# A pre-norm attention and FFN block on one core: spaced weight loads, the row maxima added by GpSimd, and a shorter lag between two passes

## The chip, the cores and the metric

The kernel runs on one core of a Trainium2 chip. The metric is the device time of the program in microseconds. Five engines work side by side, each through its own list in order: TensorE (PE in the profile, its weight loads PEld), VectorE (DVE), ScalarE (ACT), GpSimd (POOL) and SyncE (SP), which here only issues DMA transfers.

## What is computed

The reference, cut to what matters (2048 tokens, width 512, 32 heads of 16, FFN width 1792, all bf16):

```python
h  = x + attention(layernorm(x)) @ wo          # softmax(q k^T / 4) v, 32 heads
h2 = h + (gelu(layernorm(h) @ w_gate) * (layernorm(h) @ w_up)) @ w_down
```

## The kernel before

The kernel is one planned stream. A small planner (`P.op`, `P.dma`) takes the instructions in the order in which the Python code emits them, keeps for each buffer key the last writer and the readers, and puts semaphore waits where an engine needs another's result. Every engine then runs its own list strictly in the order of emission, so an instruction that waits holds up all that was emitted after it for that engine.

**Units and two passes.** The queries are cut in eight groups of 256 rows (`gi`), the heads in eight slots of four heads (`slot`), which makes 64 units. A unit has 16 ticks. In the *first pass* TensorE computes scores of 128 queries by 512 keys into PSUM, two matmuls a tick (`p1_pair`, L573), and VectorE takes the maximum of each row (`p1_consume`, L582). After a unit's last tick `negm_pre` reduces these to one negated maximum for each row and head (NEGM, L588), and GpSimd splits it into three bf16 parts in four short instructions (L592 to L595) that write the tile ST. `negm_post` transposes ST into STG by DMA (L601) and copies three rows for each of the four heads from STG into the spare rows 16 to 18 of that head's block of QT (L604, four transfers). KT holds ones in these rows, so that in the *second pass* the matmul of K by Q (`p2_pair`, L618) yields the score minus the maximum, and ScalarE only has to take the exponential (L628). Matmuls with V follow (`pv_burst`, L644).

**The order of the work.** One loop runs over ticks. In each tick it emits a first-pass pair of unit `tick // 16`, a second-pass pair of unit `(tick - P2_START) // 16`, then either matmuls with V or a piece of the "dense" stream, then what was deferred to this tick. `P2_START = 16 + LAGX`, so a unit's second pass begins LAGX ticks after the last tick of its first pass. The waits of a tick's first-pass and second-pass matmuls are gathered ahead of the first of them: TensorE starts neither before both may run. The loop ends when the second pass does; the last ticks have second-pass work alone.

**The dense stream** holds the QKV projections at the start, the end of each pair of slots (`item_ofin`: GpSimd's reciprocal of the sums, L670, and the scaling, L673), the output projection, and the FFN of each group (`item_gate`, `item_up`, `item_down`). It takes one PSUM bank at a time once `dense.single` is set, four ticks before P2_START; before that it runs at a faster rate. It is started by what the second pass has finished and keeps its own pauses in ticks. Each gate tile is copied out by ScalarE (g), GpSimd makes the inner polynomial of GELU of it (L781 to L783), ScalarE takes its tanh four or more ticks after the copy (L795), GpSimd finishes it (L786, L787) and multiplies by the up tile (L843). Seven such tiles belong to one FFN group; the last group's FFN runs after the loop.

**The FFN weights** lie where the QKV projection's buffers were. When the last projection has been emitted, `qkv_finished` emits three loads (L482 to L484, 1792 KB each) for SyncE, which wait for the readers of the old buffers.

**SyncE** issues all transfers in the order of emission. It knows nothing of ticks: it goes on as soon as the wait of its next transfer is fulfilled.

Of the kernel before, what the change touches and what calls it, by code (L numbers as in the profile page):

```python
# [189 lines left out]
ALU = mybir.AluOpType  # L190
# [6 lines left out]
GC = 0.7978845608028654  # L197

NPT = 12
LAGX = 10  # L200
PAUSE = 2


def bass_sequential_preLN__mha_block__geglu_ffn__prompt_kernel(nc, A_x, A_wqkv, A_wo, B_x, B_w_gate, B_w_up, B_w_down, out):
    dbg = None
    with ExitStack() as es:
        block = es.enter_context(nc.Block())
        P = Plan(nc, es)
# [270 lines left out]
        def qkv_finished():  # L479
            fk = [("xnT", t) for t in range(NT)] + ["wqkv"] + [(nm_, dc) for nm_ in ("wq_r", "wk_r") for dc in range(4)] + [("QKS", i_) for i_ in range(4)] + [("QKS2", i_) for i_ in range(2)]  # L480
            dF = rdeps("F", fk)
            P.dma("sp", lambda e: e.dma_start(out=wg_sb[:], in_=B_w_gate.rearrange("(c p) j -> p c j", p=128)), "wg", writes=["wg"], extra_deps=dF)  # L482
            P.dma("sp", lambda e: e.dma_start(out=wu_sb[:], in_=B_w_up.rearrange("(c p) j -> p c j", p=128)), "wu", writes=["wu"], extra_deps=dF)
            P.dma("sp", lambda e: e.dma_start(out=wd_sb[:], in_=B_w_down.rearrange("(c p) j -> p c j", p=128)), "wd", writes=["wd"], extra_deps=dF)  # L484

        qk_n = [0]
        qk_late = []
        def item_projT(b, which, ht, c):
            wr, nm = (wq_r, "wq_r") if which == "q" else (wk_r, "wk_r")
            for dc in range(4):  # L490
                P.op("pe", lambda e, dc=dc: e.matmul(pbank[:, b, :], wr[:, dc, 128 * ht:128 * ht + 128], xnT[:, dc, 512 * c:512 * c + 512], start=(dc == 0), stop=(dc == 3)),  # L491
                     reads=[(nm, dc)] + [("xnT", t) for t in range(4 * c, 4 * c + 4)], writes=[("pb", b)], sig=(dc == 3))
                if dc == 1:
                    yield 2
            si, s2 = qk_n[0] % 4, qk_n[0] % 2; qk_n[0] += 1
            def dst(slot):
                if which == "q":
                    return QT[:, c, slot, :], [("qT", slot, c)] + [("qTaug", slot, c, f_, g_) for f_ in range(2) for g_ in range(4)]
                return KT[:, slot, 512 * c:512 * c + 512], [("kT", slot, c)]
            def mask_op(src, key, slot):  # L500
                o_ap, keys = dst(slot)
                if which == "q":
                    P.op("pool", lambda e: e.tensor_scalar(out=o_ap, in0=src, scalar1=qmask[:, 0:1], scalar2=None, op0=ALU.mult), reads=[key, "qmask"], writes=keys)  # L503
                else:
                    P.op("pool", lambda e: e.tensor_scalar(out=o_ap, in0=src, scalar1=kmask[:, 0:1], scalar2=kbias[:, 0:1], op0=ALU.mult, op1=ALU.add), reads=[key, "kmask", "kbias"], writes=keys)
            p1_now = p1_begun[0]
            def direct():
                o_ap, keys = dst(2 * ht)
                if which == "q":
                    P.op("act", lambda e: e.activation(out=o_ap, in_=pbank[:, b, :], func=ACT.Copy, scale=qmask[:, 0:1]), reads=[("pb", b), "qmask"], writes=keys)  # L510
# [12 lines left out]
            qkv_left[0] -= 1  # L523
            if qkv_left[0] == 0:
                qkv_finished()
            return 2
# [38 lines left out]
        def p1_pair(ui, j, gp):  # L565
            gi, slot = units[ui]
            c, hf = gi // 2, gi % 2
            qt, kc = 2 * hf + j // 8, (j // 2) % 4
            tiles = []
            for jj in range(2):  # L570
                g = 2 * gp + jj
                b = p1_ring[0] % 3; p1_ring[0] += 1
                P.op("pe", lambda e, g=g, b=b: e.matmul(pbank[:, b, :], QT[32 * g:32 * g + 32, c, slot, 128 * qt:128 * qt + 128],  # L573
                                                        KT[32 * g:32 * g + 32, slot, 512 * kc:512 * kc + 512], start=True, stop=True, tile_position=(32 * g, 0)),
                     reads=[("qT", slot, c), ("qTaug", slot, c, hf, g), ("kT", slot, kc)], writes=[("pb", b)], sig=(jj == 1))
                tiles.append((b, j // 8, kc, g))
            return tiles

# [18 lines left out]
        def negm_post(ui):  # L597
            gi, slot = units[ui]
            c, hf = gi // 2, gi % 2
            par = ui % 2  # L600
            P.dma("sp", lambda e: e.dma_start_transpose(out=STG[:, par, :].rearrange("p (q s) -> p q s", q=2), in_=ST[:, par].rearrange("p q s -> p (q s)")),  # L601
                  ("stT", par), reads=[("ST", par)], writes=[("STG", par)])
            for g in range(4):
                P.dma("sp", lambda e, g=g: e.dma_start(out=QT[32 * g + 16:32 * g + 19, c, slot, 256 * hf:256 * hf + 256], in_=STG[32 * g + 16:32 * g + 19, par, :]),  # L604
                      ("aug", par), reads=[("STG", par)], writes=[("qTaug", slot, c, hf, g)])

        pv_pending = []
        pt_n = [0]
# [1 line left out]
        def p2_pair(ui, j, gp):  # L610
            gi, slot = units[ui]
            c, hf = gi // 2, gi % 2
            m = j // 2
            tiles = [(banks.take(), m, 2 * gp + jj) for jj in range(2)]
            for i in range(2):
                kt = 2 * m + i
                for (b, _, g) in tiles:
                    P.op("pe", lambda e, g=g, b=b, kt=kt, i=i: e.matmul(pbank[:, b, 256 * i:256 * i + 256], KT[32 * g:32 * g + 32, slot, 128 * kt:128 * kt + 128],  # L618
                                                                        QT[32 * g:32 * g + 32, c, slot, 256 * hf:256 * hf + 256], start=True, stop=True, tile_position=(32 * g, 0)),
                         reads=[("qT", slot, c), ("kT", slot, kt // 4)] + [("qTaug", slot, c, hf, g_) for g_ in range(4)], writes=[("pb", b)],  # L620
                         sig=(i == 1 and g == 2 * gp + 1))
            return tiles

# [69 lines left out]
        def add_ffn(gi):  # L693
# [3 lines left out]
            for k in range(2):  # L697
                dense.add(item_down, gi, k, est=7)

        def load_xres(gi):  # L700
            assert gi < 2 or ffn_done.get(gi - 2), "dense stream too far behind (residual reuse)"
            for k in range(2):
                P.dma("sp", lambda e, k=k: e.dma_start(out=g_h(gi, k), in_=xv[:, 2 * gi + k, :]), ("xres", gi % 2, k), writes=[("h", gi % 2, k)])
# [14 lines left out]
        def post_hnT(gi, k):  # L718
# [2 lines left out]
                  ("hnT", 2 * gp + k), reads=[("OH", 2 * gp + k)], writes=[("hnT", gp, k)])  # L721
            hn_left[gi] = hn_left.get(gi, 2) - 1
            if hn_left[gi] == 0:
                defer(3, lambda: add_ffn(gi))

        def item_oproj(b, gi, k):
            gp, t = gi % 2, 2 * gi + k
# [71 lines left out]
        def gate_up_mms(b, gi, f, w, nm):  # L799
            hT = hnT_l[gi % 2]  # L800
            hr = [("hnT", gi % 2, k) for k in range(2)]
            for i in range(2):
                fc = 2 * f + i
                for dc in range(4):
                    P.op("pe", lambda e, dc=dc, fc=fc, i=i: e.matmul(pbank[:, b, 256 * i:256 * i + 256], w[:, dc, 128 * fc:128 * fc + 128], hT[:, dc, :], start=(dc == 0), stop=(dc == 3)),  # L805
                         reads=[nm] + hr, writes=[("pb", b)], sig=(dc == 3 and i == 1))
                if i == 0:
                    yield 2

# [37 lines left out]
        def down_mm(b, gi, k, fc):  # L847
            gp = gi % 2
            P.op("pe", lambda e: e.matmul(pbank[:, b, :], GUT[:, fc, 256 * gp + 128 * k:256 * gp + 128 * k + 128], wd_sb[:, fc, :], start=(fc == 0), stop=False),  # L849
                 reads=[("GUT", fc, gp), "wd"], writes=[("pb", b)], sig=False)  # L850

        def down_last(b, gi, k):
            P.op("pe", lambda e: e.matmul(pbank[:, b, :], ident[:], g_h(gi, k), start=False, stop=True),
# [153 lines left out]
        while True:  # L1007
# [31 lines left out]
            if pv_tick:  # L1039
                pv_burst(8)  # L1040
            run_deferred(tick)
            tick += 1
        run_deferred(tick, flush=True)
        tail_mode[0] = True
# [34 lines left out]
```

## Time and profile before

| | us |
|---|---|
| median of 3 runs | 1392.69 (1392.41 to 1392.97) |
| the profiled execution, whole | 1393.8 |
| its span, from the first to the last instruction | 1392.1 |
| busy: VectorE / ScalarE / TensorE matmul / GpSimd | 1288.5 / 1235.2 / 1080.1 / 585.9 |
| VectorE's L582, 2048 times: busy / idle just before them | 1248.9 / 38.1 |
| ScalarE's L628, 2048 times: busy | 1103.8 |

The page cuts the span into 40 slices and gives the busy share of each engine in tenths. Its chain follows the work back from the last instruction to what released each step. A line of a group names the source line, engine, operation, tiles and shapes, and then busy time, mean duration and idle time of the engine before it with what ended it. A line of a timeline gives the start, the duration, the instruction, how many in a row, and in brackets the idle time before it with its releaser. Transfers show on SP's queue (SPq) with the time that the issue took. TensorE's granted clock was 0.991 of full speed over the span.

### The profile page before, as it was taken

What the parts mean: (1) busy time and instruction counts of PE and PEld (TensorE: products, weight loads), DVE (VectorE), ACT (ScalarE), POOL (GpSimd) and SP (SyncE); (2) the same over time, 40 slices, a digit from 0 to 9 for tenths busy, and PEclk for the clock granted to TensorE, in tenths of its full rate; (3) what the DMA queues carried; (4) which work ended last, traced back from release to release, by engine and by line L of the source; (5) the groups of instructions that cost most, each with busy time, mean ns of one, the idle gap of its engine ahead of it and who ended that gap; (6) DMA issues with size and microseconds to landing.
All of it is one profiled execution on the core that took longest, in us unless ns stands there. A gap on an engine that the chain in (4) does not pass through costs nothing.

```text
span 1392.1 us, 33568 instructions
## 1 busy us (share of the span) xinstructions
PE 1080.1 (78%) x12464; PEld 372.1 (27%) x12682; DVE 1288.5 (93%) x2190; ACT 1235.2 (89%) x2409; POOL 585.9 (42%) x830
## 2 busy tenths in 40 slices
PE   4977757777787778777787778777787778877787
PEld 2222212223222222222222322222222322222224
DVE  5999969999999999999999999999999999999912
ACT  4499959999999999999999999899999999999991
POOL 4446611256313562236422662146512563145611
PEclk9999989999999999999999999999999999999999
DMA  3110040100010000000001000100001000100000
GB/s 121 42 29 24 26 164 6 29 5 4 10 21 17 4 6 13 21 11 6 6 13 26 6 6 9 23 13 6 4 13 29 6 3 10 25 14 3 6 15 12
DMA packets 50096, 28.00 MB, mean 20 GB/s; under 512 B 35600, under 2 KB 48400, under 8 KB 49936
## 3 DMA queue, kind: packets, MB, share of 16 engines
q1 hardware_dynamic: 49936, 25.84, 7.0%
q8 instruction: 103, 1.69, 0.5%
q14 instruction: 57, 0.47, 0.1%
HBM read 11.80 MB, written 2.10 MB: 10 GB/s over the span
## 4 chain that ended last, share of the span: by engine, by line
DVE 72%; PE 10%; ACT 8%; issue 7%; DMA 1%; POOL 1%; SPq 1%; POOLq 0%; ACTq 0%; DVEq 0%
DVE PM L582 70%; ACT PT L628 6%; PE pbank L573 3%; PE pbank L618 2%; PE pbank L644 1%; PE pbank L805 1%; DVE NEGM L588 1%; PE pbank L491 1%; PE pbank L849 1%; DVE stats L324 1%; ACT OA L467 1%; DMA OnT<-Otok 1%; PE pbank L730 1%; SPq L604 0%; DMA STG<-ST 0%
## 5 line engine op out<-in xcount | busy, mean ns | idle before, releaser
L582 DVE TENSOR_REDUCE PM<-pbank 128x1 f32<-128x512 f32 x2048 | 1248.9, 685 | 38.1 <-PE pbank L618 26.1
L628 ACT ACTIVATE PT<-pbank 128x512 bf16<-128x512 f32 x2048 | 1103.8, 613 | 87.1 <-PE pbank L618 24.6
L573 PE MATMUL pbank<-KT,QT 32*128 32x512 bf16 x2048 | 399.8, 383 | 208.8 <-DVE PM L582 148.4
L618 PE MATMUL pbank<-QT,KT 32*128 32x256 bf16 x4096 | 401.0, 273 | 2.3 <-ACT PT L628 2.2
L573 PEld LDWEIGHTS pbank<-KT,QT 32*128 32x128 bf16 x2048 | 109.2, 91 | 592.6 <-DVE PM L582 575.0
L1001 PE MATMUL pbank<-ones_bf,ident 128*128 128x512 bf16 x651 | 213.9, 384 | 36.8 <-ACT PT L628 28.9
L644 PE MATMUL pbank<-PT,VA 128*17 128x256 bf16 x4096 | 203.7, 276 | 18.8
L592 POOL CAST ST<-NEGM 128x8 bf16<-128x8 f32 x64 | 13.9, 218 | 318.6 <-DVE NEGM L588 318.6
L670 POOL TENSOR_TENSOR LINV<-OAT,negone 128x16 f32<-128x16 f32 (+1 forms) x32 | 92.0, 2876 | 92.9 <-ACT OAT L467 67.2
L618 PEld LDWEIGHTS pbank<-QT,KT 32*128 32x128 bf16 x4096 | 114.8, 92 | 11.2 <-ACT PT L628 7.0
L644 PEld LDWEIGHTS pbank<-PT,VA 128*17 128x17 bf16 x4096 | 56.5, 87 | 147.0 <-PE pbank L644 92.4
L781 POOL TENSOR_TENSOR w_sb<-g_sb 128x512 f32<-128x512 f32 x49 | 50.9, 1039 | 105.8 <-ACT g_sb L467 105.8
L1001 PEld LDWEIGHTS pbank<-ones_bf,ident 128*128 128x128 bf16 x826 | 49.8, 97 | 100.5 <-ACT PT L628 68.1
L805 PE MATMUL pbank<-hnT_l,wg_sb 128*128 128x256 bf16 x448 | 67.9, 277 | 1.8 <-issue 0.7
L805 PE MATMUL pbank<-hnT_l,wu_sb 128*128 128x256 bf16 x448 | 67.9, 277 | 0.0
L783 POOL TENSOR_TENSOR w_sb<-w_sb,g_sb 128x512 f32<-128x512 f32 x49 | 62.1, 1268 | 4.1
L787 POOL TENSOR_TENSOR th_sb<-th_sb,g_sb 128x512 f32<-128x512 f32 x49 | 62.0, 1264 | 4.1
L843 POOL TENSOR_TENSOR GUT<-th_sb,u_sb 128x512 bf16<-128x512 f32 x49 | 62.0, 1266 | 0.5
L849 PE MATMUL pbank<-wd_sb,GUT 128*128 128x512 bf16 x202 | 56.1, 381 | 5.5 <-PE pbank L618 2.0
L503 POOL TENSOR_SCALAR QT<-QKS,qmask 128x512 bf16<-128x512 bf16 x31 | 48.2, 1562 | 27.3 <-DMA QKS<-QKS 19.5
L786 POOL TENSOR_SCALAR th_sb<-th_sb 128x512 f32<-128x512 f32 x49 | 30.2, 617 | 68.3 <-ACT th_sb L795 68.3
L805 PEld LDWEIGHTS pbank<-hnT_l,wg_sb 128*128 128x128 bf16 x448 | 36.2, 98 | 27.7 <-issue 14.0
(112 smaller groups left out, 639.2 us busy)
## 6 DMA issues: line engine op xcount, KB each, us to landing
QT<-STG SPq DMA_DIRECT2D x256, 1.5 KB
QKS<-QKS SPq DMA_DIRECT2D x32, 112.0 KB, 2.2
x_sb<-in_A_x_dram SPq DMA_DIRECT2D x4, 512.0 KB, 5.6
xres<-in_A_x_dram SPq DMA_DIRECT2D x16, 128.0 KB, 2.2
out_dram<-out_sb SPq DMA_DIRECT2D x16, 128.0 KB, 1.8
wg_sb<-in_B_w_gate_dram SPq DMA_DIRECT2D x1, 1792.0 KB, 7.2
wu_sb<-in_B_w_up_dram SPq DMA_DIRECT2D x1, 1792.0 KB, 12.1
wd_sb<-in_B_w_down_dram SPq DMA_DIRECT2D x1, 1792.0 KB, 16.6
```

The lines of the kernel that those rows point to most:

```text
L573: P.op("pe", lambda e, g=g, b=b: e.matmul(pbank[:, b, :], QT[32 * g:32 * g + 32, c, slot, 128 * qt:128 * qt + 128], KT[32 * g:32 * g + 32, ...
L582: P.op("dve", lambda e, b=b, qt=qt, kc=kc, g=g: e.tensor_reduce(out=PM[:, par, qt, kc, g:g + 1], in_=pbank[:, b, :], axis=AX.X, op=ALU.max ...
L618: P.op("pe", lambda e, g=g, b=b, kt=kt, i=i: e.matmul(pbank[:, b, 256 * i:256 * i + 256], KT[32 * g:32 * g + 32, slot, 128 * kt:128 * kt + ...
L628: P.op("act", lambda e, b=b, pi=pi: e.activation(out=PT[:, pi, :], in_=pbank[:, b, :], func=ACT.Exp), reads=[("pb", b)], writes=[("PT", pi)])
L644: P.op("pe", lambda e, g=g, kt=kt, pi=pi, slot=slot, i=i, col=col: e.matmul(pbank[32 * g:32 * g + 17, PVB, 256 * col:256 * col + 256], VA[ ...
L670: P.op("pool", lambda e: e.tensor_tensor(out=li, in0=oat4[:, :, :, 16], in1=negone[:, 0:8 * ns].rearrange("p (q h) -> p q h", q=2), op=ALU ...
L783: P.op(eng, lambda e: e.tensor_tensor(out=ws, in0=ws, in1=gs, op=ALU.mult), reads=[("w", par), ("g", par)], writes=[("w", par)])
L787: P.op(eng, lambda e: e.tensor_tensor(out=ts_, in0=ts_, in1=gs, op=ALU.mult), reads=[("th", par), ("g", par)], writes=[("th", par)])
L805: P.op("pe", lambda e, dc=dc, fc=fc, i=i: e.matmul(pbank[:, b, 256 * i:256 * i + 256], w[:, dc, 128 * fc:128 * fc + 128], hT[:, dc, :], st ...
L843: P.op("pool", lambda e: e.tensor_tensor(out=o_ap, in0=shp(ts_), in1=shp(us), op=ALU.mult), reads=[("th", par), ("u", par)], writes=o_keys ...
L849: P.op("pe", lambda e: e.matmul(pbank[:, b, :], GUT[:, fc, 256 * gp + 128 * k:256 * gp + 128 * k + 128], wd_sb[:, fc, :], start=(fc == 0), ...
L1001: P.op("pe", lambda e: e.matmul(pbank[:, b, :], ident[:], ones_bf[:, 0:512], start=True, stop=True), reads=["ident", "ones_bf"], writes=[( ...
```

## The change

Three things change together.

1. `LAGX` is 6 instead of 10.
2. The three weight loads become twelve pieces: four of the gate weights and four of the up weights (448 KB each, one for every 128 rows of the width), and four of the down weights (three of 512 KB and one of 256 KB). `qkv_finished` only lists them. The loop emits one piece at ticks 7, 9, 11 and 13 of a unit until the list is empty. The weights' keys are kept by piece, so that a matmul waits for its own. An FFN group is added to the dense stream only once all pieces are emitted.
3. The four transfers from STG into QT become one GpSimd addition of the STG tile to the unit's 256 columns of QT (128 x 256, bf16). STG is zero outside the three rows of each head, and QT is zero in these rows. The keys of QT are kept by halves of 256 columns.

```diff
-LAGX = 10
+LAGX = 6
...
-            P.dma("sp", ... out=wg_sb[:], in_=B_w_gate..., "wg", writes=["wg"], extra_deps=dF)
-            P.dma("sp", ... out=wu_sb[:], in_=B_w_up..., "wu", writes=["wu"], extra_deps=dF)
-            P.dma("sp", ... out=wd_sb[:], in_=B_w_down..., "wd", writes=["wd"], extra_deps=dF)
+            wviews = [(wg_sb, B_w_gate.rearrange("(c p) j -> p c j", p=128), "wg", 1), (wu_sb, B_w_up.rearrange("(c p) j -> p c j", p=128), "wu", 1),
+                      (wd_sb, B_w_down.rearrange("(c p) j -> p c j", p=128), "wd", 4)]
+            for (w, v, nm, step) in wviews:
+                n = w.shape[1]
+                for k in range(0, n, step):
+                    w_pieces.append((w, v, nm, k, min(n, k + step), dF))
+        def w_piece():
+            w, v, nm, k0, k1, dF = w_pieces.pop(0)
+            P.dma("sp", lambda e: e.dma_start(out=w[:, k0:k1, :], in_=v[:, k0:k1, :]), (nm, k0), writes=[(nm, k) for k in range(k0, k1)], extra_deps=dF)
...
         def negm_post(ui):
...
-            for g in range(4):
-                P.dma("sp", lambda e, g=g: e.dma_start(out=QT[32 * g + 16:32 * g + 19, c, slot, 256 * hf:256 * hf + 256], in_=STG[32 * g + 16:32 * g + 19, par, :]),
-                      ("aug", par), reads=[("STG", par)], writes=[("qTaug", slot, c, hf, g)])
+            q_ap = QT[:, c, slot, 256 * hf:256 * hf + 256]
+            P.op("pool", lambda e: e.tensor_tensor(out=q_ap, in0=q_ap, in1=STG[:, par, :], op=ALU.add), reads=[("STG", par), ("qT", slot, c, hf)], writes=[("qT", slot, c, hf)])
...
+        def add_ffn_when(gi):
+            if w_pieces or qkv_left[0]:
+                defer(1, lambda: add_ffn_when(gi))
+            else:
+                add_ffn(gi)
...
             run_deferred(tick)
+            if w_pieces and tick % 16 in (7, 9, 11, 13):
+                w_piece()
```

More of the change, by code (lines that the diff above doesn't have):

```diff
@@ L481, in qkv_finished @@
             dF = rdeps("F", fk)
-            P.dma("sp", lambda e: e.dma_start(out=wg_sb[:], in_=B_w_gate.rearrange("(c p) j -> p c j", p=128)), "wg", writes=["wg"], extra_deps=dF)
-            P.dma("sp", lambda e: e.dma_start(out=wu_sb[:], in_=B_w_up.rearrange("(c p) j -> p c j", p=128)), "wu", writes=["wu"], extra_deps=dF)
-            P.dma("sp", lambda e: e.dma_start(out=wd_sb[:], in_=B_w_down.rearrange("(c p) j -> p c j", p=128)), "wd", writes=["wd"], extra_deps=dF)
+            wviews = [(wg_sb, B_w_gate.rearrange("(c p) j -> p c j", p=128), "wg", 1), (wu_sb, B_w_up.rearrange("(c p) j -> p c j", p=128), "wu", 1),
[4 more added lines that the diff above has]
+                    w_pieces.append((w, v, nm, k, min(n, k + step), dF))
+        w_pieces = []
+        def w_piece():
+            w, v, nm, k0, k1, dF = w_pieces.pop(0)
+            P.dma("sp", lambda e: e.dma_start(out=w[:, k0:k1, :], in_=v[:, k0:k1, :]), (nm, k0), writes=[(nm, k) for k in range(k0, k1)], extra_deps=dF)
         qk_n = [0]
@@ L497, in dst @@
                 if which == "q":
-                    return QT[:, c, slot, :], [("qT", slot, c)] + [("qTaug", slot, c, f_, g_) for f_ in range(2) for g_ in range(4)]
+                    return QT[:, c, slot, :], [("qT", slot, c, f_) for f_ in range(2)]
                 return KT[:, slot, 512 * c:512 * c + 512], [("kT", slot, c)]
@@ L574, in p1_pair @@
                                                         KT[32 * g:32 * g + 32, slot, 512 * kc:512 * kc + 512], start=True, stop=True, tile_position=(32 * g, 0)),
-                     reads=[("qT", slot, c), ("qTaug", slot, c, hf, g), ("kT", slot, kc)], writes=[("pb", b)], sig=(jj == 1))
+                     reads=[("qT", slot, c, hf), ("kT", slot, kc)], writes=[("pb", b)], sig=(jj == 1))
                 tiles.append((b, j // 8, kc, g))
@@ L619, in p2_pair @@
                                                                         QT[32 * g:32 * g + 32, c, slot, 256 * hf:256 * hf + 256], start=True, stop=True, tile_position=(32 * g, 0)),
-                         reads=[("qT", slot, c), ("kT", slot, kt // 4)] + [("qTaug", slot, c, hf, g_) for g_ in range(4)], writes=[("pb", b)],
+                         reads=[("qT", slot, c, hf), ("kT", slot, kt // 4)], writes=[("pb", b)],
                          sig=(i == 1 and g == 2 * gp + 1))
@@ L723, in post_hnT @@
             if hn_left[gi] == 0:
-                defer(3, lambda: add_ffn(gi))
+                defer(3, lambda: add_ffn_when(gi))
         def item_oproj(b, gi, k):
@@ L805, in gate_up_mms @@
                     P.op("pe", lambda e, dc=dc, fc=fc, i=i: e.matmul(pbank[:, b, 256 * i:256 * i + 256], w[:, dc, 128 * fc:128 * fc + 128], hT[:, dc, :], start=(dc == 0), stop=(dc == 3)),
-                         reads=[nm] + hr, writes=[("pb", b)], sig=(dc == 3 and i == 1))
+                         reads=[(nm, dc)] + hr, writes=[("pb", b)], sig=(dc == 3 and i == 1))
                 if i == 0:
@@ L849, in down_mm @@
             P.op("pe", lambda e: e.matmul(pbank[:, b, :], GUT[:, fc, 256 * gp + 128 * k:256 * gp + 128 * k + 128], wd_sb[:, fc, :], start=(fc == 0), stop=False),
-                 reads=[("GUT", fc, gp), "wd"], writes=[("pb", b)], sig=False)
+                 reads=[("GUT", fc, gp), ("wd", fc)], writes=[("pb", b)], sig=False)
         def down_last(b, gi, k):
```

## The prediction

> **What bounds the kernel now.** I read the page first, then the chain, then the waits and timelines of the engines where the change acts.
>
> ```profile
> DVE  5999969999999999999999999999999999999912
> DVE 72%; PE 10%; ACT 8%; issue 7%; DMA 1%; POOL 1%; SPq 1%; POOLq 0%; ACTq 0%; DVEq 0%
> L582 DVE TENSOR_REDUCE PM<-pbank 128x1 f32<-128x512 f32 x2048 | 1248.9, 685 | 38.1 <-PE pbank L618 26.1
> ```
>
> VectorE carries the chain with the 2048 maxima of the first pass (0.61 us each, two a tick: a tick is 1.2 us). A lull of VectorE between the first and last of them is lost for good; there are 38.1 us of these. The 6 in the sixth slice is the largest.
>
> ```profile
> 177.09 12.04 DVE L582 TENSOR_REDUCE PM<-pbank 128x1 f32<-128x512 f32 x20
> 200.30 1.29 DVE L582 TENSOR_REDUCE PM<-pbank 128x1 f32<-128x512 f32 x2 [11.17 <-PE pbank L618]
> ```
>
> ```profile
> 178.68 0.50 SPq L484 DMA_DIRECT2D wd_sb<-in_B_w_down_dram  x1
> 179.28 10.83 SPq L601 DMA_TRANSPOSE STG<-ST  x1
> 195.68 2.86 SPq L604 DMA_DIRECT2D QT<-STG  x4
> ```
>
> The first is VectorE's timeline, the second SyncE's. Behind 5,376 KB of weights, unit 6's transpose lands at 195.68 instead of 2.35 us after its issue; its second pass waits, and the first pass, next in TensorE's order, with it.
>
> The third place is GpSimd around the end of a unit with FFN work (timelines of GpSimd, of ScalarE, and of all engines for NEGM and the first-pass pairs):
>
> ```profile
> 646.89 0.22 POOL L592 CAST ST<-NEGM 128x8 bf16<-128x8 f32 x1 [4.35 <-DVE NEGM L588]
> 647.75 0.23 POOL L595 TENSOR_TENSOR ST<-R,ST 128x8 bf16<-128x8 f32 x1
> ...
> 649.85 2.91 POOL L670 TENSOR_TENSOR LINV<-OAT,negone 128x16 f32<-128x16 f32 x1
> 652.84 0.62 POOL L673 TENSOR_TENSOR Otok<-OAT,LINV 128x256 bf16<-128x256 f32 x1
> 653.41 1.27 POOL L843 TENSOR_TENSOR GUT<-th_sb,u_sb 128x512 bf16<-128x512 f32 x1
> 654.64 1.04 POOL L781 TENSOR_TENSOR w_sb<-g_sb 128x512 f32<-128x512 f32 x1
> 655.77 0.62 POOL L782 TENSOR_SCALAR w_sb<-w_sb 128x512 f32<-128x512 f32 x1
> 656.47 1.26 POOL L783 TENSOR_TENSOR w_sb<-w_sb,g_sb 128x512 f32<-128x512 f32 x1
> ```
>
> ```profile
> 647.81 0.42 ACT L467 ACTIVATE OAT<-pbank 128x272 f32<-128x272 f32 x1
> 659.90 0.67 ACT L795 ACTIVATE th_sb<-w_sb 128x512 f32<-128x512 f32 x1
> ```
>
> ```profile
> 646.35 0.39 PE L573 MATMUL pbank<-KT,QT 32*128 32x512 bf16 x2 [0.29 <-ACT PT L628]
> 646.62 0.21 DVE L588 TENSOR_REDUCE NEGM<-PM 128x8 f32<-128x32 f32 x1
> 651.18 0.39 PE L573 MATMUL pbank<-KT,QT 32*128 32x512 bf16 x2
> ```
>
> NEGM starts at 646.62, after the pair of the next unit's first tick; 651.18 is the pair four ticks on. GpSimd goes straight on after L595; L783 ends at 657.73, and the tanh that reads it runs at 659.90: 2.2 us to spare. ScalarE is busy 18.9 to 19.7 us of such a 20 us unit (windows), so it has no room for a wait.
>
> I sum against the profiled execution: span 1392.1 us, 1393.8 us in all; the median of the runs is 1392.69, and the sum is carried over to that. No difference below 0.2% (2.8 us) counts as seen.
>
> **Second pass six steps behind.** The loop has 1024 + 16 + LAGX ticks, so four go. They leave the drain, where only second-pass ticks remain: 26 of them from 1325.2 to 1354.3, 1.12 us each, set by ScalarE. Four make **-4.5 us**. Everything tied to the second pass (exponentials, heads' ends, FFN) moves four ticks earlier against NEGM; the pattern mod 4 is kept. QKV projections get fewer double-speed ticks (18 instead of 22); following the code they end near tick 120 instead of 108, still ahead of their use.
>
> **Twelve pieces.** The stall goes: NEGM 6 to NEGM 7 is 31.73 us where the units beside it take 19.58 and 19.37, so **-12.2 us**. The spacing in ticks doesn't pace SyncE, which isn't held by ticks: after a unit's transpose it issues the next four pieces at once. At the rate of the three loads (5,376 KB from 177.7 to about 195) a burst of four takes a third of that, 5.8 us, behind the transpose and gone before the next, 19.4 us later. They cost nothing under that cover; the last leaves near NEGM 9 + 3 = 250, and the first gate matmul reads at 279.2. Put ahead of a transpose, a burst would cost 5.8 less the 2.3 us of slack found below. The Trainium skill (DMA: Bandwidth & Descriptors, Rules for kernel authors) asks for transfers of 1 MiB or more and for small ones to be joined, which speaks against this cut; the row that bears on it is the 11.17 us, where large transfers in a row were the harm, and followed blindly the rule would leave the 12.2 us in place.
>
> **Add instead of four transfers.** Before, the four L604 transfers took 2.76 us of issue after the landing, then landed; 256 issues leave SyncE. Now: transpose landed at NEGM + 3.72, then one add. No row shows a 128x256 add of bf16. L673 (128x256, two inputs) took 0.62; below stands half of L505 (128x512 bf16, 0.77), 0.39; above L503 (1.56 for 128x512 bf16), half of it 0.78 by width, all of it if each input costs that much. I take 0.62, the nearest in shape. With 0.09 from release to start (as for L503 and L505) the rows are ready at NEGM + 4.45. TensorE wants them six ticks after the pair that NEGM follows by 0.53: 6 x 1.22 - 0.53 = 6.8. Slack 2.3 us: no loss in an ordinary unit. The Trainium skill (GPSIMD Engine Reference, Engine selection) would have VectorE do an elementwise add, GpSimd being about twice as slow on two inputs; with the 0.42 us of VectorE's own 128x256 copy, that would put 64 x 0.42 = 27 us on the engine that carries the chain, against 0.62 us each on one busy 42%.
>
> The add's wait is what costs. GpSimd now stands from L595 (NEGM + 1.4) to NEGM + 4.45 in each of 64 units, with all FFN and normalisation work queued behind. I put the before's rows four ticks earlier against NEGM and queue them again. Of the seven tanhs of an FFN group five keep room. Two don't:
>
> - The tanh of 659.90. NEGM now follows the pair of 651.18, at 651.7. L670 is ready at 648.23, so L670, L673 and L843 (3.0 + 0.57 + 1.27, start to start) come first and end at NEGM + 1.4. The four NEGM steps start 1.16 late, the add ends at 5.6, and L781 to L783 (3.09) end at 8.7. The tanh was due at 659.90 - 651.7 = 8.2: it waits 0.57.
> - The tanh of 680.09. NEGM follows the pair of 671.37 by 0.26. L786 and L787 (1.96) now stand behind the add: 4.47 + 1.96 + 3.09 = 9.55, with release 9.62, due at 680.09 - 671.63 = 8.46: it waits 1.16.
>
> A wait of ScalarE goes on in full: ticks with a tanh already last 1.53 instead of 1.23, TensorE waiting for banks, and late next is VectorE. 1.73 x 7 groups = **+12.1 us** (0 if all were absorbed).
>
> Transposes land 0.55 to 1.8 us late in 12 of the 64 units (mean 1.18), when a 16 KB instruction fetch is on the DMA engines. That was covered; now it adds to those two tanhs: 14 units x 12/64 x 1.18 = **+3.1** (0 to 5.1, the sum over the units of these two places that were late before). Units 1 and 2 had the NEGM steps 2.65 and 2.23 us late behind masks, landings at 7.04 and 5.95; plus 0.7 that is up to 0.9 beyond 6.8: **+0.5**.
>
> Sum: -4.5 - 12.2 + 12.1 + 3.1 + 0.5 = -1.0, so 1391.7 us.
>
> **Rivals.**
> Faster: the tanhs are held little, since the add is quick (0.39 takes 14 x 0.23 = 3.2 off) or a wait is absorbed by idle time of ScalarE (0.9 us in a 20 us unit). For it: two of three terms are rows, not estimates. Against: 659.90 has an exponential right before and after. With half the 12.1 + 3.1 it gives 1384; with none, 1376.5.
>
> Slower: the same place, with an add at L503's rate for each input, 1.56 us. Each of the 14 tanhs waits 0.94 more: +13.2, 1404.9. It decides from an add of about 0.88 us ((2.8 + 1.0)/14 above 0.62). For it: L503 is bf16 in and out, as the add is. Against: L505 and L673.
>
> The change doesn't do what it says: pieces get ahead of a transpose anyway, since SyncE isn't paced. Three units at 5.8 - 2.3 = 3.5 us, 1402.2.
>
> **Numbers.** Near-cancellation 0.42, by itself 1389.9 to 1395.5; faster 0.30; the slow add and other slowing on GpSimd 0.24; pieces ahead of transposes 0.04. So 0.30 faster, 0.42 within 0.2%, 0.28 slower. For 8 in 10 the range leaves out the full absorption and the full slow add: 1383.5 to 1400.
>
> **What would show it.** VectorE's sixth slice at 9 and no lull of 11 us; a drain of 22 ticks, about 24.6 us; GpSimd waiting for the STG landing some 2.4 us in 64 units; ScalarE's L795 waiting for GpSimd's L783 fourteen times, 12 to 15 us in all, and VectorE's idle time before L582 near 38 - 12 + 14 = 40 us. L795 without a wait, or the add far from 0.62, would make me wrong; so would TensorE's L618 or L573 waiting for the add.

## The result: a little slower, and the profile after

| | before | after |
|---|---|---|
| median of 20 runs each, us | 1392.37 (1389.90 to 1395.73) | 1395.57 (1392.65 to 1402.17) |
| profiled execution, us (its span) | 1393.8 (1392.1) | 1395.23 (1393.5) |
| VectorE's maxima: idle before them, us | 38.1 | 45.2 |
| granted TensorE clock over the span | 0.991 | 0.989 |

The ratio is 1.0024 (1.0016 to 1.0033): slower by 0.24%, where no measurable change was forecast. Lines of the code move down: L582 is now L590, L588 L596, L592 L600, L601 L609, L618 L625, L783 L796, L786 L799, L795 L808. The addition is L612. Some experiments stand one line lower from L612 on (L626, L636, L797, L809).

The page of after, VectorE's slices, the chain and two groups:

```profile
DVE  5899999999999999999999989999999999999932
...
DVE 67%; PE 9%; ACT 8%; issue 5%; POOL 5%; DMA 4%; SPq 0%; POOLq 0%; ACTq 0%; DVEq 0%
...
L590 DVE TENSOR_REDUCE PM<-pbank 128x1 f32<-128x512 f32 x2048 | 1249.9, 682 | 45.2 <-PE pbank L625 32.7
...
L612 POOL TENSOR_TENSOR QT<-QT,STG 128x256 bf16<-128x256 bf16 x64 | 42.8, 669 | 163.7 <-DMA STG<-ST 163.7
```

The 6 in the sixth slice is a 9: the stall over the weights is gone. The last slice but one has 3 instead of 1: the maxima go on closer to the end, so the drain is shorter. But VectorE's idle time before the maxima has risen, GpSimd and DMA have 5% and 4% of the chain where they had 1% each, and the addition takes 0.67 us and is waited for 2.56 us on the average (163.7 / 64).

The stall's place, VectorE's and then SyncE's timeline of after:

```profile
177.08 10.93 DVE L590 TENSOR_REDUCE PM<-pbank 128x1 f32<-128x512 f32 x18
188.19 8.59 DVE L590 TENSOR_REDUCE PM<-pbank 128x1 f32<-128x512 f32 x14 [0.18 <-PE pbank L625]
```

```profile
179.60 1.19 SPq L609 DMA_TRANSPOSE STG<-ST  x1
180.90 8.24 SPq L524 DMA_DIRECT2D QKS<-QKS  x3
192.62 1.30 SPq L492 DMA_DIRECT2D wg_sb<-in_B_w_gate_dram  x3
198.22 1.20 SPq L609 DMA_TRANSPOSE STG<-ST  x1
199.46 0.57 SPq L492 DMA_DIRECT2D wg_sb<-in_B_w_gate_dram  x1
200.08 2.68 SPq L492 DMA_DIRECT2D wu_sb<-in_B_w_up_dram  x2
```

The lull of 11.17 us is 0.18. The pieces go in bursts, and each burst is issued well before a transpose or right behind one; the transpose issued at 198.22 is not late (its rows land 3.77 us after NEGM, as in an ordinary unit).

The waits of after, one row each of ScalarE, GpSimd and VectorE (us in all, times, longest):

```profile
ACT th_sb L808 <- POOL w_sb L796: 10.5, 14, 2.4
```

```profile
POOL QT L612 <- DMA STG<-ST: 163.7, 64, 4.0
```

```profile
DVE PM L590 <- PE pbank L625: 32.7, 77, 2.9
```

The tanh waits for GpSimd fourteen times, two in each of seven FFN groups, as foretold. The longer of the two, in unit 30 (GpSimd's timeline, then one row of ScalarE's):

```profile
660.16 0.23 POOL L603 TENSOR_TENSOR ST<-R,ST 128x8 bf16<-128x8 f32 x1
662.84 0.67 POOL L612 TENSOR_TENSOR QT<-QT,STG 128x256 bf16<-128x256 bf16 x1 [2.44 <-DMA STG<-ST]
663.47 0.62 POOL L799 TENSOR_SCALAR th_sb<-th_sb 128x512 f32<-128x512 f32 x1
664.17 1.27 POOL L800 TENSOR_TENSOR th_sb<-th_sb,g_sb 128x512 f32<-128x512 f32 x1
665.40 1.04 POOL L794 TENSOR_TENSOR w_sb<-g_sb 128x512 f32<-128x512 f32 x1
666.53 0.62 POOL L795 TENSOR_SCALAR w_sb<-w_sb 128x512 f32<-128x512 f32 x1
667.23 1.27 POOL L796 TENSOR_TENSOR w_sb<-w_sb,g_sb 128x512 f32<-128x512 f32 x1
```

```profile
668.53 0.63 ACT L808 ACTIVATE th_sb<-w_sb 128x512 f32<-128x512 f32 x1 [0.85 <-POOL w_sb L796]
```

GpSimd stands for 2.44 us on the transpose; everything after it in its list is ready and late; ScalarE, full in this unit, then waits 0.85.

**Where the time went**, by NEGM to NEGM of the two profiles. Unit 6 to 7 takes 19.86 instead of 31.73 (-11.9). The last NEGM is nevertheless 7.65 us later (1333.43 against 1325.78), so the FFN units gave back 19.5. From the last NEGM on, after is 6.2 shorter: the last exponential ends 24.35 after it instead of 28.93 (-4.6), and the tail behind is 1.65 shorter. Together +1.4 between the two profiled executions.

### The profile page after: what moved, and what is told of

Its sections match the earlier page's. It is cut to its first block, busy times and chain, and to the rows that moved or that the text cites. A ratio compares the mean times of both kernels' runs of the same rounds, so it can differ in the third digit from the quotient of the medians.

```text
span 1393.5 us, 33501 instructions
## 1 busy us (share of the span) xinstructions
PE 1122.0 (81%) x12666; PEld 369.5 (27%) x12666; DVE 1289.0 (92%) x2190; ACT 1235.5 (89%) x2409; POOL 631.3 (45%) x894
## 4 chain that ended last, share of the span: by engine, by line
DVE 67%; PE 9%; ACT 8%; issue 5%; POOL 5%; DMA 4%; SPq 0%; POOLq 0%; ACTq 0%; DVEq 0%
DVE PM L590 65%; ACT PT L635 7%; PE pbank L581 3%; PE pbank L625 2%; DMA STG<-ST 2%; DMA OnT<-Otok 2%; PE pbank L818 1%; DVE NEGM L596 1%; PE pbank L651 1%; PE pbank L862 1%; PE pbank L1014 1%; POOL w_sb L796 1%; PE pbank L743 1%; DVE stats L324 1%; POOL th_sb L800 1%
## 5 line engine op out<-in xcount | busy, mean ns | idle before, releaser
L590 DVE TENSOR_REDUCE PM<-pbank 128x1 f32<-128x512 f32 x2048 | 1249.9, 682 | 45.2 <-PE pbank L625 32.7
L625 PE MATMUL pbank<-QT,KT 32*128 32x256 bf16 x4096 | 403.8, 275 | 1.6 <-ACT PT L635 1.5
L1014 PE MATMUL pbank<-ones_bf,ident 128*128 128x512 bf16 x810 | 254.0, 390 | 4.6 <-ACT PT L635 2.1
L625 PEld LDWEIGHTS pbank<-QT,KT 32*128 32x128 bf16 x4096 | 115.1, 92 | 9.6 <-ACT PT L635 5.9
L612 POOL TENSOR_TENSOR QT<-QT,STG 128x256 bf16<-128x256 bf16 x64 | 42.8, 669 | 163.7 <-DMA STG<-ST 163.7
L600 POOL CAST ST<-NEGM 128x8 bf16<-128x8 f32 x64 | 14.1, 220 | 169.8 <-DVE NEGM L596 168.7
L1014 PEld LDWEIGHTS pbank<-ones_bf,ident 128*128 128x128 bf16 x810 | 49.1, 97 | 100.8 <-ACT PT L635 76.3
L796 POOL TENSOR_TENSOR w_sb<-w_sb,g_sb 128x512 f32<-128x512 f32 x49 | 62.2, 1269 | 4.1
L862 PE MATMUL pbank<-wd_sb,GUT 128*128 128x512 bf16 x224 | 61.0, 382 | 2.8 <-PE pbank L625 0.2
L799 POOL TENSOR_SCALAR th_sb<-th_sb 128x512 f32<-128x512 f32 x49 | 30.4, 620 | 67.7 <-ACT th_sb L808 67.7
L511 POOL TENSOR_SCALAR QT<-QKS,qmask 128x512 bf16<-128x512 bf16 x31 | 48.3, 1565 | 13.8 <-ACT QKS L467 7.0
```

The source lines that it names most:

```text
L590: P.op("dve", lambda e, b=b, qt=qt, kc=kc, g=g: e.tensor_reduce(out=PM[:, par, qt, kc, g:g + 1], in_=pbank[:, b, :], axis=AX.X, op=ALU.max ...
L796: P.op(eng, lambda e: e.tensor_tensor(out=ws, in0=ws, in1=gs, op=ALU.mult), reads=[("w", par), ("g", par)], writes=[("w", par)])
L1014: P.op("pe", lambda e: e.matmul(pbank[:, b, :], ident[:], ones_bf[:, 0:512], start=True, stop=True), reads=["ident", "ones_bf"], writes=[( ...
```

## The experiments

The comparison runs of the kernel before that went with these had medians of 1391.5 and 1391.9; ratios are against them. Unless said otherwise a kernel starts from after.

**One part of the three alone: the pieces.** `LAGX = 10` and the four transfers as before.

```diff
-LAGX = 6
+LAGX = 10
...
-            P.op("pool", ... tensor_tensor(out=q_ap, in0=q_ap, in1=STG[:, par, :], op=ALU.add) ...)
+            for g in range(4):
+                P.dma("sp", ... out=QT[32 * g + 16:32 * g + 19, ...], in_=STG[32 * g + 16:32 * g + 19, par, :] ...)
```

> Of the three changes only the twelve weight pieces; the four transfers of L604 and LAGX 10 as before. Theory (the terms of the changed kernel's sum stand by themselves): the lull of 11.2 us in unit 6 goes and nothing else changes, so 1392.4 - 11.9 = 1380.5 us, VectorE's idle time before its maxima 38 - 12 = 26 us, no tanh waits for GpSimd. Rival (the pieces cost something where they share the DMA engines with transposes): 1384 us or more, and transposes of units 7 to 9 that land more than 1 us late.

Measured 1378.14 (1376.75 to 1380.63), ratio 0.9906 (0.9894 to 0.9919). Units 24 to 31 take 159.13 us as before (159.11), and L809 waits for nothing. The pieces are worth over 13 us by themselves; the other two parts together cost 17 (after stands 17.4 above this run).

**Is it the cut or the spacing?** The same, but three whole loads, one at tick 7 of each unit.

```diff
-wviews = [(wg_sb, ..., "wg", 1), (wu_sb, ..., "wu", 1), (wd_sb, ..., "wd", 4)]
+wviews = [(wg_sb, ..., "wg", 4), (wu_sb, ..., "wu", 4), (wd_sb, ..., "wd", NFC)]
...
-            if w_pieces and tick % 16 in (7, 9, 11, 13):
+            if w_pieces and tick % 16 == 7:
```

> e1_pieces with the three whole loads, one in each of three units, instead of twelve pieces. Theory (what counts is that no transpose stands behind more than the queue can clear before it is needed, not the size of a transfer): the same time as e1_pieces within 1.5 us, 1377 to 1380, and no lull of VectorE above 1.5 us between 50 and 1300 us except by an output projection. Rival (the size counts): a lull of some 3 to 6 us in one of units 7 to 9.

Measured 1379.15 (1378.56 to 1379.95), ratio 0.9911 (0.9894 to 0.9927): the same as twelve pieces. What harmed was three loads in a row ahead of a transpose, not their size.

**Without GpSimd's wait.** The addition is emitted one tick later, so that what stands behind NEGM's four steps runs first, in two forms: always (the first), or only once the QKV projections are done (the second).

```diff
-            P.op("pool", ... add ...)
+            defer(1, lambda: P.op("pool", ... add ...))
```

> The changed kernel, with the add one tick later in GpSimd's list (deferred by one tick), so that FFN work stands ahead of it instead of behind it; the add's own 0.67 us stays. Theory (it is GpSimd's standing at the add that holds the tanhs): the 14 waits of L808 (10.5 us) go, and with them the half-clock stretches that follow the long ones; TensorE may wait 0.2 to 0.4 us for the add in the unit before the seventh of each eight; 1395.6 - 10 to 14 = 1382 to 1386 us. Rival (it is the additional work on GpSimd, or its accesses, 64 x 0.67 us): no change, 1394 us or more. Rival (the lag of six is too short for the rows): TensorE's waits take the place of the tanhs', 1392 us or more.

Measured 1385.01 (1380.26 to 1387.81), ratio 0.9951 (0.9937 to 0.9965). L808 has no wait left. But TensorE waited three times for the addition, in units 1, 5 and 6; in 5 and 6 (1.48 and 2.35 us) it now stood behind QKV masks (L511, 1.56 us each), one of which itself stood waiting for a transfer (the waits of TensorE):

```profile
PE pbank L581 <- POOL QT L612: 4.2, 3, 2.3
```

```diff
-            P.op("pool", ... add ...)
+            add = lambda: P.op("pool", ... add ...)
+            defer(1, add) if qkv_left[0] == 0 else add()
```

> The changed kernel with the add one tick later in GpSimd's list, but only from the end of the QKV projections on; in e2_add_later the same delay put the add behind masks of 1.56 us in units 4 to 6, and TensorE waited 4.2 us for it there. Theory: those waits go and the tanhs' don't come back: 1385.0 - 4.2 = 1380.8 us, 1378 to 1382; no wait of L808 for L796; TensorE's clock never at one half between 50 and 1320 us, or once. Rival (the delay itself costs elsewhere): 1384 us or more.

Measured 1379.38 (1378.36 to 1382.15), ratio 0.9912 (0.9898 to 0.9925). Against after this is 16 us, for one tick's difference in the place of one instruction. The rows of L808's waits are gone, and TensorE's clock is full from 41 us to 1375 of the span's 1376.6 us, where after has six stretches at half before its last NEGM.

**More of the wait.** A second GpSimd instruction behind the addition (QT times ones, 128 x 256):

```diff
+            P.op("pool", ... tensor_tensor(out=q_ap, in0=q_ap, in1=ones_bf[:, 0:256], op=ALU.mult) ...)
```

> The changed kernel with a second GpSimd operation of the same size right behind the add (QT times ones, 0.67 us), for which the second pass waits too. Theory: each of the 14 late tanhs waits 0.67 us more, 9.4 us, and longer waits tip TensorE's clock to one half more often (some 0.8 us each time, in up to 14 places): 1395.6 + 9.4 to 1395.6 + 20 = 1405 to 1416 us; waits of L808 some 20 us in all. The second pass has 6.9 - 5.2 = 1.7 us of slack left in ordinary units, so TensorE doesn't wait for the rows there. Rival (the standing doesn't matter, the loss lies elsewhere): below 1398 us.

Measured 1411.33 (1409.57 to 1415.55), ratio 1.0147 (1.0133 to 1.0162): 15.8 above after. ScalarE's row:

```profile
ACT th_sb L809 <- POOL w_sb L797: 20.1, 14, 3.2
```

The waits rose by 9.6 us, the time by more; the stretches at half clock between 41 us and the last NEGM went from six to eleven.

**Six or ten steps.** After, and then the version with the later addition, with

```diff
-LAGX = 6
+LAGX = 10
```

> The changed kernel with LAGX 10 again; pieces and GpSimd's add stay. Theory: the drain gets four ticks longer (+4.5). Queued again as for the prediction, FFN rows now stand otherwise to NEGM: in the unit that has L677, L680 and L856 behind the add the tanh is due at NEGM + 13.3 and its polynomial ends at 4.5 + 1.96 + 3.0 + 0.6 + 1.3 + 3.1 = 14.4, so one wait of about 1.0 us a group where the lag of 6 has 0.16 and 0.85; so that the waits stay near 7 us. If the rest of the loss (0.7 us a group of units without a wait, three ticks with a tanh that now lie away from NEGM) comes from the lag, it goes: -4.8. In all 1395 us, 1393 to 1397. Rival (the short lag is what costs, through the rows' lateness): 1395.6 + 4.5 - 14 = 1386 us and no waits of L808.

Measured 1409.10 (1404.26 to 1412.39), ratio 1.0124 (1.0107 to 1.0142), far above what was expected. ScalarE's row:

```profile
ACT th_sb L808 <- POOL w_sb L796: 19.9, 14, 2.5
```

With ten steps two tanhs of each group wait again: the one foretold, in unit 29 of the group looked at (0.84 us), and one in unit 28 that I had not queued, 0.84 us too in a group whose transposes land in time. That makes 1.68 a group, 11.8 in seven, instead of 1.01. The other 8.2 us of the row follow transposes that land late in seven of these fourteen units; unit 28 itself waits 2.3, since its transpose lands 5.2 us after NEGM instead of 3.7. Ten stretches at half clock followed. What the addition's wait costs is set by which FFN instructions happen to stand behind it, and by where the late transposes fall.

> e9_later_ffn with LAGX 10. Two terms act against each other: the drain is four ticks longer (+4.5 us), and three tanhs of each FFN group stand again just ahead of NEGM, where VectorE has 0.2 us of other work while TensorE waits for ScalarE's banks (-0.6 to -0.7 us a group, seven groups: -4.1 to -4.8). Theory (the shorter lag by itself is worth nothing here): the same time as e9_later_ffn within 1.5 us, units 24 to 31 together 159.1 us as in the kernel before (159.8 with the lag of 6), and the drain 28.9 us after the last NEGM instead of 24.4. Rival (the lag is worth its four ticks): 4 us slower than e9_later_ffn.

Measured 1377.69 (1376.20 to 1377.89), ratio 0.9893 (0.9878 to 0.9908): the lowest median here, 14 us below the runs of before beside it and 18 below after. It is not apart from the pieces alone (1378.14, with overlapping runs and intervals): the addition, well placed, neither gains nor costs. With no tanh waiting, ten steps are as good as six: the drain is 4.6 us longer (last exponential 28.94 after the last NEGM against 24.35), and each FFN group is shorter (units 24 to 31: 159.12 against 159.74). So the shorter lag, by itself, brings nothing. The next fences show why: VectorE and then ScalarE of before around the second tanh of the group, and the same of the later addition at lag six.

```profile
621.33 4.92 DVE L582 TENSOR_REDUCE PM<-pbank 128x1 f32<-128x512 f32 x8
626.28 0.21 DVE L588 TENSOR_REDUCE NEGM<-PM 128x8 f32<-128x32 f32 x1
626.49 3.71 DVE L582 TENSOR_REDUCE PM<-pbank 128x1 f32<-128x512 f32 x6
```

```profile
624.76 0.67 ACT L795 ACTIVATE th_sb<-w_sb 128x512 f32<-128x512 f32 x1
```

```profile
605.48 4.92 DVE L590 TENSOR_REDUCE PM<-pbank 128x1 f32<-128x512 f32 x8
610.64 3.71 DVE L590 TENSOR_REDUCE PM<-pbank 128x1 f32<-128x512 f32 x6 [0.24 <-PE pbank L626]
```

```profile
608.92 0.67 ACT L809 ACTIVATE th_sb<-w_sb 128x512 f32<-128x512 f32 x1
```

A tanh takes ScalarE 0.67 us beside two exponentials, which holds TensorE for a bank and makes VectorE idle 0.20 to 0.25 us some 1.7 us later. In before three of seven fall 18 us or more after a NEGM, as this one does: the next NEGM's 0.21 us then lies where the gap would be, and nothing is lost. With the lag of six they fall at 13.2, 13.2, 3.5, 13.8, 8.3, 18.4 and 8.7 us after a NEGM, and one is covered.

**Moving the tanhs back.** The version with the later addition, lag six, with all FFN groups but the last two begun four ticks later.

```diff
-                defer(3, lambda: add_ffn_when(gi))
+                defer(7 if gi < GL - 1 else 3, lambda: add_ffn_when(gi))
```

> e9_later_ffn, with each FFN group but the last two started four ticks later, so that its tanhs stand to NEGM as they did with the lag of 10, while the drain keeps its 22 ticks. Theory (the lost 0.2 us are a matter of where tanhs lie against NEGM): units 24 to 31 take 159.1 us again, 3 to 4 us less than e9_later_ffn over five groups, 1375 to 1378 us. Rival (the 0.7 us a group comes from the add or the lag itself): the same as e9_later_ffn.

Measured 1379.74 (1379.29 to 1381.00), ratio 0.9913 (0.9899 to 0.9926): no gain. The FFN began nine to ten ticks later, not four, since the dense stream had other items first; two tanhs were covered (18.4 and 18.9 us after NEGM) and units 24 to 31 took 159.54. That lies between the other two and agrees with the reading, but the experiment didn't do what it was made for.

**The addition on VectorE**, four ticks later.

```diff
-            P.op("pool", ... add ...)
+            defer(4, lambda: P.op("dve", ... add ...))
```

> The changed kernel with the add on VectorE instead of GpSimd, emitted four ticks later, when the transposed maxima have landed, so that VectorE doesn't stand. Theory (VectorE carries the chain, an add there is all loss, GpSimd's waits go): 64 adds of 0.2 to 0.42 us, 13 to 27 us on top of a kernel without waits (1380): 1393 to 1407 us, no wait of L808 for L796. Rival (VectorE has room while it waits for TensorE, or the add is so short there that it is the better place): below 1388 us.

Measured 1395.02 (1389.58 to 1397.19), ratio 1.0017 (1.0004 to 1.0031). It takes 0.28 us there (median), less than half of GpSimd's 0.67. No tanh waits; yet it is 15.6 us above the later addition on GpSimd. In the profiles an ordinary group of eight units (48 to 55) is 1.15 us longer than there, 0.14 a unit, about half of the addition's length. The rest lies in single units (2.21 in unit 28, which has 6.8 us at half clock; 1.49 in unit 1) and in the tail behind the drain (1.5), so the 15.6 is not the price of the additions alone.

**The four transfers with a shorter lag.** The pieces alone, as in the first experiment, with a lag of 8 and then of 6:

```diff
-LAGX = 10
+LAGX = 8    # the second: 6
```

> The twelve pieces, the four transfers, LAGX 8: the rows land about 8 us after NEGM, wanted at 6.9 + 2.4 = 9.3, so TensorE doesn't wait. Two ticks less of drain than e1_pieces: -2.2 us. The tanhs of an FFN group then lie at 16, 16, 6, 16, 11, 1 and 11 us after a NEGM, none in the last 2 us of a unit, where three of seven lay with the lag of 10. Theory (a tanh costs 0.2 to 0.25 us of VectorE's time unless it falls there): +0.7 us a group, units 24 to 31 together 159.8 to 160.1 instead of 159.1, +5 to +7 over seven groups, in all 1381 to 1383 us, slower than e1_pieces in spite of the shorter drain. Rival (the lag gives its ticks): 1376 us, units 24 to 31 together 159.1.

> The twelve pieces and LAGX 6, with the four transfers into QT instead of GpSimd's add. Theory: GpSimd doesn't stand, no tanh waits; but the rows of QT land some 8 us after NEGM (last issue at 5.9, about 2.2 to land) and the second pass wants them at 6.9, so TensorE waits 1.1 to 1.4 us in each of 64 units (70 to 90 us), and more where TensorE's clock falls to one half after the wait: 1440 to 1490 us. Rival (the transfers would have been ready in time, the add was not needed for the lag): below 1385 us.

Measured 1487.45 (1484.66 to 1491.28) and 1527.63 (1517.75 to 1531.67), ratios 1.0691 (1.0670 to 1.0711) and 1.0967 (1.0925 to 1.1009). Both lie above what was expected, the first by over 100 us, the second by 38. With the lag of six TensorE does wait for the rows of QT as foretold, though in 31 units (mean 1.8 us) and not in all; a second wait, for the output projection's transposes (OnT), was not foreseen, and 36 stretches at half clock, 171 us of them, lie before the last NEGM. TensorE's waits:

```profile
PE pbank L581 <- DMA QT<-STG: 55.7, 31, 3.8
PE pbank L744 <- DMA OnT<-Otok: 29.3, 7, 4.9
```

Where the second comes from (SyncE's timeline with the lag of six, and the row of TensorE's):

```profile
606.66 1.19 SPq L609 DMA_TRANSPOSE STG<-ST  x1
608.99 2.76 SPq L612 DMA_DIRECT2D QT<-STG  x4
611.79 0.89 SPq L717 DMA_DIRECT2D xres<-in_A_x_dram  x2
612.73 2.53 SPq L724 DMA_TRANSPOSE OnT<-Otok  x2
```

```profile
615.39 1.03 PE L744 MATMUL pbank<-wo_sb,OnT 128*128 128x512 bf16 x2 [4.09 <-DMA OnT<-Otok]
```

The transposes for the output projection stand behind the four transfers on SyncE and come too late now that it is due four ticks earlier against NEGM: TensorE waits 4.09 us and then runs at half clock (1.03 us for two matmuls that take 0.61 otherwise). With the lag of eight, where no wait was expected, the same two rows of TensorE's read 32.6 us in 17 units and 27.5 in 7. Of the 16.2 us that units 24 to 31 take more than with the lag of ten, 10.3 lie in units 25 and 26, around the output projection, and 4.9 in units 28 and 29, with the rows' waits. There the rows of QT are late because GpSimd is; its timeline around the NEGM of 592.93:

```profile
591.90 2.90 POOL L678 TENSOR_TENSOR LINV<-OAT,negone 128x16 f32<-128x16 f32 x1 [17.05 <-ACT OAT L467]
594.88 0.62 POOL L681 TENSOR_TENSOR Otok<-OAT,LINV 128x256 bf16<-128x256 f32 x1
595.44 0.22 POOL L600 CAST ST<-NEGM 128x8 bf16<-128x8 f32 x1
```

Two steps are not a multiple of four, so the heads' ends fall on the NEGM, and its four steps begin 2.5 us after it here, and 3.4 and 3.8 in units 28 and 29, instead of 0.3 (median over units 8 to 59: the transpose is issued 2.79 after NEGM, where it was 1.40). The four transfers are what needs the lag of ten; the addition is what makes six possible at all. One change prepares the other, and neither pays.

**Keeping the clock up.** After, with one more of the kernel's filler matmuls (L1014) in each tick that has room.

```diff
-            if not pv_tick and (cost or 0) < 2:
-                dummy(banks.free[0], 2 - (cost or 0))
+            if not pv_tick and (cost or 0) < 3:
+                dummy(banks.free[0], 3 - (cost or 0))
```

> The changed kernel with one more filler matmul (0.2 us of TensorE) in each tick without matmuls by V, so that TensorE has done more when a wait comes. Theory (after a wait of about 0.9 us and more, TensorE's clock is at one half for 3.4 or 6.8 us when too little was done in such a stretch, and that adds 0.45 us for each 3.4): half-clock stretches between 50 and 1320 us fall from six to at most two, the tanhs' waits stay at 9 to 11 us, 1392 to 1394 us. Rival (TensorE has no room for it; a tick has some 0.26 us of waiting left): VectorE waits for TensorE in most ticks, 1410 us or more.

Measured 1403.54 (1401.49 to 1405.58), ratio 1.0086 (1.0071 to 1.0101): slower than after by 8 us, so missed. The filler did hold the clock (three stretches at half between 41 and 1340 us instead of six, all in units whose transpose landed 5.2 us or more after NEGM). But it holds the ticks of the first unit, which have no second pass, at 1.5 us: NEGM 8 comes 4.9 us later than in after; the other 3 us were not traced. Two units can be compared cleanly, 22 and 46, which have the same tanh wait and transpose in both: 21.73 and 21.83 us in after, with half clock, 21.28 and 21.28 here, at full clock.

## Why the prediction was wrong, step by step

**Twelve pieces: right.** -12.2 was forecast, -11.9 measured between the profiles, and by the pieces alone a little more. The rival in which bursts get ahead of transposes did not occur: they went in bursts, as said, but beside them.

**The drain: right.** -4.5 forecast, -4.6 measured. The tail behind it gave another -1.65 that I had not: before's profile has a stretch of half clock there (1368.6 to 1372.0) and after's none.

**The addition: right in price.** 0.67 us against 0.62; slack against the second pass as figured (TensorE never waited for it). The slow rival, decided from 0.88, falls. The Trainium skill (GPSIMD Engine Reference, Engine selection) puts GpSimd at about twice VectorE's time for two inputs; 0.67 against 0.28 agrees roughly. With the addition on VectorE the kernel took as long as after (1395.02 and 1395.57) and 15.6 us more than with the later addition on GpSimd: the quicker engine is the one that has no time to spare. The 0.42 us that I had put for VectorE is the row of an f32 copy; the bf16 copy of the same size (0.29 us) was the nearer one. The +0.5 for units 1 and 2 did not come: they took 19.55 and 19.60 us against 19.56 and 19.56.

**The two tanhs: mechanism right, size too large.** 12.1 + 3.1 = 15.2 was forecast, 10.5 measured. GpSimd's chain ended where I put it (9.51 us after NEGM against 9.62), but the tanhs fell due later: 0.16 and 0.85 in an undisturbed group instead of 0.57 and 1.16, so 7.1 for seven groups. The late transposes cost 3.4 (units 38, 45 and 62), near the 3.1.

**What was costed at nothing.** The step that failed is "Everything tied to the second pass ... moves four ticks earlier against NEGM; the pattern mod 4 is kept", from which I took the drain as pure gain. Moving the FFN against NEGM takes two of three tanhs from under NEGM: units 24 to 31 are longer by 1.01 for the two waits and by 0.67 beyond them (160.79 - 159.11 = 1.68). Seven groups make +4.7, all that the drain gave. That the lag is worth nothing without the waits is shown by the pair of the later addition, 1379.38 at six and 1377.69 at ten. That the loss is the NEGM cover is read from the gaps (six of 0.20 to 0.25 us a group against four, which make 0.41 of it, smaller ones some 0.1); moving the tanhs back, which would have shown it, did not come off.

**The clock was not in the sum at all.** After, three windows around the wait of unit 22 (us, then each engine's busy time, granted clock, DMA share, GB/s), and TensorE's timeline across it:

```profile
501.60:508.40 6.80, 4.76 (x64) 1.46 (x64) 6.21 (x11) 5.73 (x12) 6.54 (x7) 1.00 0.01 2
508.40:511.80 3.40, 3.25 (x22) 0.70 (x22) 2.38 (x4) 2.99 (x7) 3.21 (x4) 0.50 0.00 0
511.80:518.60 6.80, 6.01 (x74) 1.72 (x72) 6.68 (x12) 5.83 (x12) 0.00 (x0) 1.00 0.00 0
```

```profile
506.43 0.86 PE L651 MATMUL pbank<-PT,VA 128*17 128x256 bf16 x16
508.55 0.61 PE L581 MATMUL pbank<-KT,QT 32*128 32x512 bf16 x2 [1.26 <-ACT PT L635]
```

A tanh's 0.85 us becomes 1.26 us without a matmul, and then TensorE runs at half clock for 3.4 us, in which VectorE is busy 2.38 us. The unit loses 1.25 instead of the 0.81 that the same wait costs in unit 30, where the clock holds. There are six such stretches, two of them of 6.8 us. The five in units 22, 38, 45, 46 and 62 cost about 3.7 together (each unit against an undisturbed one plus its wait); the sixth, in unit 57, has its equal in before's unit 41.

**The sum again**, between the profiles: -11.9 - 4.6 - 1.65 + 10.5 + 4.7 + 3.7 = +0.8, measured +1.4; 0.6 is spread over units and was not traced. Two missing terms of 8.4 were mostly covered by waits that came out 4.7 smaller and the tail's 1.65. The rest of the way to the medians' +3.2 is the profiled execution of before, which lay 1.4 above its median, while I carried the sum to the median as if it were typical; in its unit 41 alone it lost 2.15 us.

Of the signs named beforehand, the full slice, the drain of 24.4, GpSimd's 64 waits and the fourteen waits of the tanh came true, these last with 10.5 us in all instead of 12 to 15; VectorE's idle time before the maxima was to be 40 us and is 45.2, and that is where the two missing terms (the tanhs' places and the clock) show.

## What to carry to other kernels

Put an instruction that waits for a transfer as late in an in-order list as its reader allows: here one tick later, behind work that was ready, was worth 16 us. Before counting a shorter pipeline lag as gain, list which short operations it moves out from under others and which queue order each lag brings with it; here every lag had a different set of victims, and only a trial showed them. And try the parts of a combined change one by one: the best of this one was the weights' spacing, while the shorter lag needed the addition, and the addition's wait cost more than the lag saved.

## What was not expected of the hardware

A wait of TensorE of 1.2 to 1.3 us in an otherwise busy stretch was enough to bring the granted clock to 0.50 for 3.4 or 6.8 us (four of after's six stretches; before the other two it waited 2.8 and 2.5), at a cost of some 0.45 us for 3.4. Not each wait did so: of seven tanh waits of 0.85 us or more in the same place of the seven groups, four. The number of stretches went with the waits of the tanh: none to two without any (none in the later addition's second form, two in before, one of them behind the stall over the weights), six with 10.5, ten and eleven with 19.9 and 20.1; the two runs with the four transfers and a short lag, where TensorE waits for other things, stand apart.

Which waits do it can be read from the traces. The starts of after's six stretches (508.42, 832.68, 976.04, 996.52, 1214.98, 1320.79) lie whole multiples of 3.413 us apart. Cut into windows on that grid, the six windows just ahead of the stretches are those in which TensorE was least busy, 0.64 to 1.93 us, and every other full-clock window between 45 us and the last NEGM has 2.00 us or more (units 22 and 30: window, its length, TensorE's busy time and the rest):

```profile
505.01:508.42 3.41, 1.91 (x30) 0.48 (x24) 2.80 (x5) 2.56 (x6) 3.24 (x4) 1.00 0.00 0
668.84:672.25 3.41, 2.00 (x16) 0.52 (x16) 2.07 (x4) 3.27 (x8) 3.25 (x4) 1.00 0.00 0
```

TensorE's wait is 1.26 us long in both; 1.13 us of it lie inside the window in unit 22, and 0.95 in unit 30, where the rest falls into the window before. In all runs here, in the same stretch of the kernel, each window with less than 1.75 us was followed by half clock and none with more than 2.05; between these it went either way (the addition on VectorE has one of 1.8 that was not followed by it and one of 2.05 that was).

The Trainium skill (TensorE: Matmul & The Clock Gate, Part 1) puts the fall to half clock after at least one idle window of about 3.4 us, and would have allowed these waits; the traces show shorter ones doing it, and the measurement decides. That a wait tips the clock only where it leaves too little work in a window would also explain why after's runs spread over 9.5 us and before's over 5.8; this is argued, not shown.
